# Nineteen columns a head: queries and keys of a Hedgehog attention relative to their last feature

## The chip, the cores and the metric

The kernel runs on one core of a Trainium2 chip. The metric is device time in microseconds (us) of one execution, the median over runs; lower is better. A core has five engines with an instruction stream each: PE (TensorE, matrix products, with its weight loads listed as PEld), DVE (VectorE), ACT (ScalarE), POOL (GpSimd) and SP (SyncE, which issues the DMA transfers here). Work passes through SBUF (on-chip memory of 128 partitions) and PSUM (where matrix products are summed).

## The reference

Two layers, each an attention (A) and a dense network (B) with a normalization ahead and a residual behind, on x of 2048 rows by 640 columns, 32 heads of 20 columns, 1536 hidden columns, all in float32:

```python
def _A_ref(x, wqkv, w_phi, wo):
    qkv = transpose((x @ wqkv).reshape(B, S, 3, H, Dh), 2, 0, 3, 1, 4)
    q, k, v = qkv[0], qkv[1], qkv[2]
    pq = einsum("bhsd,hdf->bhsf", q, w_phi)
    pk = einsum("bhsd,hdf->bhsf", k, w_phi)
    phi_q = concatenate([softmax(pq), softmax(-pq)], axis=-1)
    phi_k = concatenate([softmax(pk), softmax(-pk)], axis=-1)
    kv = einsum("bhsf,bhsd->bhfd", phi_k, v)
    z  = einsum("bhsf->bhf", phi_k)
    num = einsum("bhqf,bhfd->bhqd", phi_q, kv)
    den = einsum("bhqf,bhf->bhq", phi_q, z)[..., None] + 1e-6
    return (num / den) @ wo
def _B_ref(x, w1, b1, w2):
    h = x @ w1 + b1
    return (h * tanh(softplus(h))) @ w2
for _ in range(2):
    x = x + _A_ref(layernorm(x), ...)
    x = x + _B_ref(layernorm(x), ...)
```

The softmax runs over a head's 20 features. It doesn't change when one number is added to all of them, and neither does the softmax of the negated features.

## The kernel before

**Tiles and precision.** The 2048 rows are 16 tiles of 128, two tiles to a block, eight blocks. The 640 columns are contracted in five steps of 128 (`KD`). Each operand of a large product is split into a high part that TensorE takes in its faster float32 form (fp32r) and the remainder, and each product is three matmuls: high by high, high by low, low by high. A row of 640 outputs is made in two halves of 320 columns (`HC`), each in its own PSUM bank. The weights are the moving operand of these matmuls, so a half moves 320 columns past a stationary 128 by 128 tile of the normalized rows.

**Folding.** At the start of layer 1 `w_phi` is multiplied into the weights of queries and keys, so that no product with `w_phi` is left in the loops. The heads' 20 by 20 matrices stand as blocks of six on a diagonal of `bd`, 120 wide; `fold_part` (L244) multiplies a stretch of the raw weights by such a block, and `fold_end` (L250, L251) splits the sum into the high and low weights. The folded weights are written to `wp_d` in DRAM (L205, L206) and read back for layer 2 (L194, L200).

**First pass** (`attend_first`, over the eight blocks). For each block six projections run in the order k0, k1, v0, v1, q0, q1: keys, values and queries of the block's two tiles, 30 matmuls each (`project_half`, L364). What follows a projection is a generator that is advanced by one step after each later projection:

- `features` turns a projection into the two softmaxes: ACT copies it out of PSUM into the second half of each head's 40 columns in tile `e` (L381, listed under the helper's line L129); DVE takes maximum and minimum per head (L388); one subtraction makes the first half (L389, on POOL for queries, on DVE for keys) and one the second (L391, DVE); ACT takes the exponential in place; DVE sums (L397) and inverts (L398); POOL multiplies (L399).
- Keys are then multiplied with the values (L436) into one PSUM bank that sums over all blocks.
- Queries are transposed by DVE (L444) and written to `e_d` in DRAM by four transfers (L448).

Key tiles come from the pool `big` with five buffers, shared with other uses. Query tiles are two fixed buffers (`query_tile`, shown as r210 and r211, or r in a row), so the copy of a query waits until the writes to `e_d` of the query two tiles before have landed. The projections take PSUM tiles `mm` (two of them) or `one` (four). In layer 1 the block's two halves of normalized rows are also transposed by TensorE; in layer 2 they arrive transposed from DRAM.

**Second pass** (`attend_second`). The last query tile is projected in `rest`, between other work. `load` (L597) reads a block's features back from `e_d`; `average` (L637) multiplies them with the product of keys and values; the output projection runs again through `project_half` (L364), here with `wo`, after which come the residual and the statistics for the next normalization.

**Dense network** (`dense`). Hidden products move 256 columns (L759), Mish runs on ACT, DVE and POOL, and the second product moves 320 (L801).

**Order.** A scheduler decides the order of instructions on each engine from its own simulated timeline, with priority by the written order. The start of layer 1 (all engines) and the second pass (PE and SP) keep the written order. Copies made through `act` keep their order among themselves. POOL, DVE, ACT and SP each run their streams in order, so an instruction that waits holds what stands behind it on its engine.

Of the kernel before, what the change touches and what calls it, by code (L numbers as in the profile page):

```python
# [8 lines left out]
F32 = mybir.dt.float32  # L9
F32R = mybir.dt.float32r  # L10
AF = mybir.ActivationFunctionType
ALU = mybir.AluOpType
# [4 lines left out]
P = 128  # L17
S = 2048
D = 640
F = 1536  # L20
H = 32
DH = 20
KD = D // P
KF = F // P
BT = 2
# [2 lines left out]
NT = S // P  # L28
G = 11
HC = D // 2  # L30
EW = 2 * D
GW = 3 * (DH + 1)
VW = H * (DH + 1)
# [8 lines left out]
def kernel(  # L42
# [13 lines left out]
    nc = tc.nc  # L56
# [6 lines left out]
    dram = ctx.enter_context(tc.tile_pool(name="dram", bufs=1, space=DRAM))  # L63
# [36 lines left out]
    stats = const.tile([P, NB, 2, BT], F32, name="stats")  # L100


    wp_d = dram.tile([2, 2, KD, P, D], F32, name="wp_d")

    e_d = [dram.tile([EW, BLK], F32, name=f"e_d{b}") for b in range(NB)]

# [83 lines left out]
    def load_q_weights():  # L190
        ws = [r2_pair(k) for k in range(KD)]
        for k in range(KD):
            for s in range(2):
                nc.sync.dma_start(ws[k][s].bitcast(F32), wp_d[0, s, k])  # L194
        return ws

    def load_k_weights(kv_ws):
        for k in range(KD):
            for s in range(2):
                nc.sync.dma_start(kv_ws[k][s][:, :D].bitcast(F32), wp_d[1, s, k])  # L200

    def spill_qk_weights(kv_ws, q_ws):
        for k in range(KD):
            for s in range(2):
                nc.sync.dma_start(wp_d[1, s, k], kv_ws[k][s][:, :D].bitcast(F32))  # L205
                nc.sync.dma_start(wp_d[0, s, k], q_ws[k][s].bitcast(F32))  # L206

    def make_five(j, rows, low=nc.gpsimd):

# [30 lines left out]
    def fold_part(ps, k, t, bd, raw):  # L240

        r, rows = raw[t]
        n = 120 * (t % 3) if t < 5 else 200
        nc.tensor.matmul(ps[:, n:n + rows], r[:rows, k * P:(k + 1) * P], bd[:rows, t, :rows],  # L244
                         start=True, stop=True)

    def fold_end(ws, ps, k, c):
        n0, n1 = (0, 360) if c == 0 else (360, D)
        hi, lo = ws[k][0][:, n0:n1], ws[k][1][:, n0:n1]
        nc.scalar.activation(hi, ps[:, :n1 - n0], AF.Copy)  # L250
        nc.vector.tensor_tensor(lo, ps[:, :n1 - n0], hi.bitcast(F32), op=ALU.subtract)  # L251
# [94 lines left out]
        return Transposed(cols=cols)  # L346


    def project(xts, t, ws, col, ps=None):

        if ps is None:
            mm = mm_tile()
            ps = [mm[:, 0], mm[:, 1], mm]
        for c in range(2):
            project_half(ps[c], xts, t, ws, col, c)
        return ps

    def project_half(ps, xts, t, ws, col, c, ks=range(KD)):
        sl = slice(t * P, (t + 1) * P)
        cs = slice(col + c * HC, col + (c + 1) * HC)  # L360
        for k in ks:
            h, l, wh, wl = xts.hs[k], xts.ls[k], ws[k][0][:, cs], ws[k][1][:, cs]
            for n, (a, r) in enumerate(((h, wh), (h, wl), (l, wh))):
                nc.tensor.matmul(ps[:, :HC], a[:, sl], r, start=(k == 0 and n == 0),  # L364
                                 stop=(k == KD - 1 and n == 2))

    def both(ps):

        return ps[2][:, :, :HC]


    def query_tile(i):
# [2 lines left out]
    def features(ps, e, pool_sub):  # L375

        eg = e.rearrange("p (g d) -> p g d", d=DH)
        eh = e.rearrange("p (h s d) -> p s h d", s=2, d=DH)
        ec = e.rearrange("p (c h s d) -> p s c h d", c=2, s=2, d=DH)[:, 1]
        if len(ps) > 2:  # L380
            act(ec, both(ps).rearrange("p c (h d) -> p c h d", d=DH), AF.Copy)  # L381
        else:
            for c in range(2):
                act(ec[:, c], ps[c][:, :HC].rearrange("p (h d) -> p h d", d=DH), AF.Copy)
        yield
        m = work.tile([P, 2, H], F32, tag="m", name="m", bufs=2)
        for s, op in ((0, ALU.max), (1, ALU.min)):
            nc.vector.tensor_reduce(m[:, s], eh[:, 1], axis=AX.X, op=op)  # L388
        (nc.gpsimd if pool_sub else nc.vector).tensor_tensor(  # L389
            eh[:, 0], eh[:, 1], m[:, 0].unsqueeze(2).to_broadcast([P, H, DH]), op=ALU.subtract)  # L390
        nc.vector.tensor_tensor(eh[:, 1], m[:, 1].unsqueeze(2).to_broadcast([P, H, DH]), eh[:, 1],  # L391
                                op=ALU.subtract)
        yield
        act(e, e, AF.Exp)
        yield
        r = work.tile([P, 2 * H], F32, tag="r", name="r", bufs=2)
        nc.vector.tensor_reduce(r, eg, axis=AX.X, op=ALU.add)  # L397
        nc.vector.reciprocal(r, r)  # L398
        nc.gpsimd.tensor_tensor(eg, eg, r.unsqueeze(2).to_broadcast([P, 2 * H, DH]), op=ALU.mult)  # L399
        yield  # L400
# [6 lines left out]
    def attend_first(layer, x_src, first):  # L407
# [17 lines left out]

        def keys(xts, i, v):
            e = big_tile()
            yield from features(project(xts, i % BT, kv_ws, 0), e, False)
            yield
            if i % BT == 0 and BT < i < NT - BT:  # L430
                yield
            for r in range(9):
                for j in range(4):
                    h = 3 * (4 * (r // 3) + j) + r % 3
                    if h < H:
                        nc.tensor.matmul(kva[32 * j:32 * j + DH + 1, 40 * r:40 * r + 40],  # L436
                                         v[:, (DH + 1) * h:(DH + 1) * (h + 1)], e[:, 40 * h:40 * h + 40],
                                         start=(i == 0 and r == 0), stop=(i == NT - 1), skip_group_check=True)

        def queries(xts, i, ps=None):  # L440
            e = query_tile(i)
            yield from features(project(xts, i % BT, q_ws, 0) if ps is None else ps, e, True)

            nc.vector.transpose(e, e)  # L444
            b, t = divmod(i, BT)
# [20 lines left out]
        if first is None:  # L466
            with written():
# [6 lines left out]
                nc.sync.dma_start(bd[:40, 5, :40], phi_bd[80:120, 4, 80:120])  # L474
                nc.sync.dma_start(bd[40:80, 5, 40:80], phi_bd[:40, 5, :40])
                nc.sync.dma_start(bd[:, 3:5], phi_bd[:, 3:5])
                raw_q += load_raw(0, range(3, 6))
                kv_ws = [r1_pair(k) for k in range(KD)]
                raw_v = [fetch_v(k) for k in range(KD)]
# [1 line left out]
                early = fetch(x_src, 1)  # L481
                mvs = [norm_stats(t, xt) for t in range(BT)]
                norm_scale(0, mvs)

                q_ws = [r2_pair(k) for k in range(KD)]
                mm = [mm_tile(), mm_tile()]
# [18 lines left out]
                fold_end(q_ws, pcs[4], 4, 0)  # L505
                mm = mm_tile()
                q0 = [mm[:, 0], mm[:, 1], mm]
                project_half(q0[0], nxt, 0, q_ws, 0, 0)

                def make_v(k):  # L510
                    split(kv_ws[k][0][:, D:2 * D], kv_ws[k][1][:, D:2 * D], raw_v[k])
# [1 line left out]
                for k in range(KD):  # L513
# [3 lines left out]
                    fold_end(q_ws, ps, k, 1)  # L517
                    if k > 0:
                        make_v(k - 1)
                project_half(q0[1], nxt, 0, q_ws, 0, 1)  # L520
                make_v(KD - 1)
            nc.sync.dma_start(mask, bass.AP(tensor=head_mask.tensor, offset=head_mask.offset,
                                            ap=[[1, 120], [120 * (DH + 1), 3]]))
# [48 lines left out]
        def rest():  # L572

            ps = [one_tile(), one_tile()]
            project_half(ps[0], xts, 1, q_ws, 0, 0)
            advance()
            advance()
            yield
            project_half(ps[1], xts, 1, q_ws, 0, 1, range(3))
            yield  # L580
            project_half(ps[1], xts, 1, q_ws, 0, 1, range(3, KD))
            pending.append(queries(xts, NT - 1, ps))
            next(pending[-1])
            while pending:
                yield
                advance()
# [376 lines left out]
```

## Time and profile before

| | us |
|---|---|
| median of 3 runs | 1377.01 |
| lowest and highest | 1376.39, 1379.66 |
| span of the profiled execution | 1375.0 |
| mean granted clock of TensorE | 0.999 |

The span is counted from the first to the last instruction of one execution; the runs' times hold a little more around it. By stage, from the busy times by stretches (us):

| stretch | what runs | length | PE busy | DVE busy | ACT busy | POOL busy |
|---|---|---|---|---|---|---|
| 0 to 43 | start: loads, folding, first tiles | 43.0 | 37.2 | 28.5 | 19.3 | 8.4 |
| 43 to 280 | layer 1, first pass | 237.0 | 236.6 | 194.9 | 96.3 | 109.5 |
| 280 to 364 | layer 1, second pass | 84.0 | 84.0 | 58.5 | 22.1 | 34.9 |
| 364 to 690 | layer 1, dense | 326.0 | 326.0 | 265.6 | 164.6 | 76.2 |
| 690 to 955 | layer 2, first pass | 265.0 | 262.9 | 228.9 | 101.1 | 113.9 |
| 955 to 1040 | layer 2, second pass | 85.0 | 85.0 | 56.9 | 24.3 | 34.5 |
| 1040 to 1375 | layer 2, dense | 335.0 | 330.5 | 240.1 | 153.8 | 63.6 |

The borders are chosen by eye from the timeline; passes overlap at them by some microseconds.

Rows of the profile are read like this. A group row gives the line in the kernel, the engine, the operation, the output and inputs by name, their shapes, the count (x), then the busy time, the mean of one in ns, and the engine's idle time just before with what ended most of it. A timeline row begins with the start in us and the length in us; a count at its end says that several like instructions follow each other, and the length is that of the whole run; square brackets give the idle time before it. In the chain of waits a row gives start, length and what ran then. Matmuls are pipelined: the mean of one matmul in a group is longer than the distance from one to the next.

### The profile page before, as it was taken

The numbers are of one execution on the slowest core, as the hardware profiler recorded it, in microseconds if no ns is written. First come the engines' busy times: TensorE is split into PE (matmuls) and PEld (weight loads), VectorE is DVE, ScalarE is ACT, GpSimd is POOL, SyncE is SP. The second block draws the span as 40 slices with busy tenths as digits, with TensorE's granted clock in tenths as the row PEclk, the third lists the DMA queues.
The fourth block names the chain that finished last, engine by engine and source line by source line (L and its number), as shares of the span: only waits on it lengthen the run. The fifth ranks groups of instructions, "written<-read, shape, count | busy, mean of one in ns | idle before, by whom it ended". The sixth has DMA issues, their size and how long they took to land.

```text
span 1375.0 us, 30860 instructions
## 1 busy us (share of the span) xinstructions
PE 1362.1 (99%) x12896; PEld 1349.8 (98%) x12896; DVE 1073.3 (78%) x1822; ACT 581.3 (42%) x970; POOL 441.0 (32%) x334
## 2 busy tenths in 40 slices
PE   9999999999999999999999999999999999999998
PEld 8999999999999999999999999999999999999998
DVE  5898877886688887788769899988678776677775
ACT  4344443222454545545444334332235444454443
POOL 1345553354322222122235434444242111111112
PEclk9999999999999999999999999999999999999999
DMA  9443424788614442244473433368975221333200
GB/s 337 148 95 62 75 40 96 204 242 292 224 55 97 116 105 77 59 107 99 141 245 77 85 59 64 67 132 270 285 253 151 77 59 41 94 97 96 69 29 20
DMA packets 350469, 169.85 MB, mean 124 GB/s; under 512 B 287209, under 2 KB 323801, under 8 KB 350329
## 3 DMA queue, kind: packets, MB, share of 16 engines
q1 hardware_dynamic: 350329, 167.88, 45.2%
q8 instruction: 101, 1.65, 0.5%
q14 instruction: 39, 0.32, 0.1%
HBM read 104.92 MB, written 62.91 MB: 122 GB/s over the span
## 4 chain that ended last, share of the span: by engine, by line
PE 96%; DMA 1%; DVE 1%; ACT 0%; issue 0%; DVEq 0%; SPq 0%
PE mm L364 29%; PE one L759 24%; PE mm L801 24%; PE one L364 12%; PE mm L637 3%; PE one L300 2%; PE one L436 2%; DMA v<-in_wv 1%; DMA r1l<-wp_d 0%; DVE r1l L251 0%; DVE bn L270 0%; ACT xn L129 0%; DVE r L397 0%; DVE xt L811 0%; ACT r L129 0%
## 5 line engine op out<-in xcount | busy, mean ns | idle before, releaser
L801 PE MATMUL mm<-r2h,ol 128*128 128x320 f32 x1280 | 305.0, 309 | 0.0
L785 POOL TENSOR_TENSOR ol<-big,ol 128x512 fp32r<-128x512 f32 (+1 forms) x98 | 129.9, 1326 | 483.7 <-ACT ol L784 409.3
L759 PE MATMUL one<-xtl,r1h 128*128 128x256 f32 x960 | 268.2, 279 | 0.0
L759 PE MATMUL one<-xth,r1l 128*128 128x256 f32 x960 | 268.0, 279 | 0.0
L759 PE MATMUL one<-xth,r1h 128*128 128x256 f32 x960 | 265.9, 279 | 0.0
L801 PEld LDWEIGHTS mm<-r2h,ol 128*128 128x128 f32 x1280 | 219.2, 188 | 0.3 <-ACT ol L784 0.3
L801 PE MATMUL mm<-r2l,ol 128*128 128x320 f32 x640 | 197.3, 309 | 0.0
L364 PE MATMUL mm<-r1h,xth 128*128 128x320 f32 x600 | 187.6, 313 | 1.6 <-DVE r1l L251 1.6
L364 PE MATMUL mm<-r1l,xth 128*128 128x320 f32 x600 | 185.8, 310 | 0.0
L364 PE MATMUL mm<-r1h,xtl 128*128 128x320 f32 x600 | 185.6, 310 | 0.0
L759 PEld LDWEIGHTS one<-xtl,r1h 128*128 128x128 f32 x960 | 180.4, 188 | 0.0
L759 PEld LDWEIGHTS one<-xth,r1l 128*128 128x128 f32 x960 | 180.4, 188 | 0.0
L759 PEld LDWEIGHTS one<-xth,r1h 128*128 128x128 f32 x960 | 179.6, 188 | 0.0
L774 DVE TENSOR_SCALAR big<-big 128x512 f32<-128x512 f32 (+1 forms) x98 | 57.1, 583 | 110.0 <-ACT big L772 109.8
L399 POOL TENSOR_TENSOR r<-r,r 128x1280 f32<-128x1280 f32 x32 | 77.7, 2429 | 156.4 <-DVE r L398 141.8
L801 PEld LDWEIGHTS mm<-r2l,ol 128*128 128x128 f32 x640 | 120.2, 188 | 0.0
L776 ACT ACTIVATE big<-big,two 128x512 f32<-128x512 f32 (+1 forms) x98 | 70.1, 716 | 116.1 <-DVE big L775 116.0
L772 ACT ACTIVATE big<-one,b1s 128x256 f32<-128x256 f32 x192 | 80.9, 468 | 89.0 <-PE one L759 88.5
L784 ACT ACTIVATE ol<-big 128x512 fp32r<-128x512 f32 (+1 forms) x98 | 60.9, 622 | 136.0 <-DVE big L783 135.9
L364 PEld LDWEIGHTS mm<-r1h,xth 128*128 128x128 f32 x600 | 112.8, 188 | 2.6 <-DVE r1l L251 1.8
L364 PEld LDWEIGHTS mm<-r1h,xtl 128*128 128x128 f32 x600 | 112.7, 188 | 0.2
L364 PEld LDWEIGHTS mm<-r1l,xth 128*128 128x128 f32 x600 | 112.8, 188 | 0.0
(133 smaller groups left out, 3119.9 us busy)
## 6 DMA issues: line engine op xcount, KB each, us to landing
e_d<-r SPq DMA_DIRECT2D x128, 160.0 KB, 4.0
big<-e_d SPq DMA_DIRECT2D x32, 640.0 KB, 7.6
x_d<-xt SPq DMA_DIRECT2D x23, 640.0 KB, 3.9
xt<-x_d SPq DMA_DIRECT2D x22, 640.0 KB, 5.5
n_d<-xn SPq DMA_DIRECT2D x176, 80.0 KB, 2.2
xt<-in_x SPq DMA_DIRECT2D x16, 640.0 KB, 4.4
xn<-x_d SPq DMA_DIRECT2D x28, 320.0 KB, 4.4
v<-n_d SPq DMA_DIRECT2D x30, 256.0 KB, 3.1
```

Source lines behind the costliest of these rows:

```text
L300: nc.tensor.transpose(ps[:, c, t * P:(t + 1) * P], self.rows[t][:, (c0 + c) * P:(c0 + c + 1) * P], ident)
L364: nc.tensor.matmul(ps[:, :HC], a[:, sl], r, start=(k == 0 and n == 0), stop=(k == KD - 1 and n == 2))
L399: nc.gpsimd.tensor_tensor(eg, eg, r.unsqueeze(2).to_broadcast([P, 2 * H, DH]), op=ALU.mult)
L436: nc.tensor.matmul(kva[32 * j:32 * j + DH + 1, 40 * r:40 * r + 40], v[:, (DH + 1) * h:(DH + 1) * (h + 1)], e[:, 40 * h:40 * h + 40], start ...
L637: nc.tensor.matmul(po[64 * q:64 * q + 64, c, GW * j:GW * j + w], phs[g][:n, s0:s0 + 64], kvb[:n, g, :w], start=True, stop=True)
L759: nc.tensor.matmul(ph[:, j, :], l, r, start=(n == 0), stop=(n == 3 * KD - 1))
L772: exps[0] = nc.scalar.activation(part(ta, 0)[:, j - js.start], ph[:, j, :], AF.Exp, bias=b1s[:, 2 * pr + j:2 * pr + j + 1]).ins
L774: nc.vector.tensor_scalar_min(e, e, E_CAP)
L776: nc.scalar.activation(r, n, AF.Ln, bias=two)
L784: nc.scalar.activation(ah[:, js], n, AF.Copy)
L785: nc.gpsimd.tensor_tensor(al[:, js], n, ah[:, js].bitcast(F32), op=ALU.subtract)
L801: nc.tensor.matmul(pys[t][:, c, :HC], l[:, j, sl], r, start=(f == 0 and n == 0), stop=(f == KF - 1 and n == 2))
```

## The change

Queries and keys are made with 19 columns a head (`DL`) in place of 20: 608 in place of 640 columns (`QK`), 304 in place of 320 a half (`QC`). Each is the feature less the head's twentieth feature, and the twentieth entry, which is zero by that, is set by a memset. By the invariance above both softmaxes stay what they were. For that, the last column of each head's block of `w_phi` is subtracted from the others on POOL (`shift_phi`, three calls), the folding multiplies by the first 19 columns, and the folded weights, their copies in DRAM and the projections of queries and keys are 608 columns wide. `features` sets the twentieth column of each head in tile `e` to zero on POOL and copies 19 columns a head behind it. From maximum and minimum on, 20 columns a head are worked on as before. Values, the output projection and the dense network keep their widths.

```diff
@@ -20,6 +20,7 @@
 F = 1536
 H = 32
 DH = 20
+DL = DH - 1
 KD = D // P
 KF = F // P
 BT = 2
@@ -28,6 +29,8 @@
 NT = S // P
 G = 11
 HC = D // 2
+QK = H * DL
+QC = QK // 2
 EW = 2 * D
 GW = 3 * (DH + 1)
 VW = H * (DH + 1)
@@ -100,7 +103,7 @@
     stats = const.tile([P, NB, 2, BT], F32, name="stats")
 
 
-    wp_d = dram.tile([2, 2, KD, P, D], F32, name="wp_d")
+    wp_d = dram.tile([2, 2, KD, P, QK], F32, name="wp_d")
 
     e_d = [dram.tile([EW, BLK], F32, name=f"e_d{b}") for b in range(NB)]
 
@@ -191,19 +194,19 @@
         ws = [r2_pair(k) for k in range(KD)]
         for k in range(KD):
             for s in range(2):
-                nc.sync.dma_start(ws[k][s].bitcast(F32), wp_d[0, s, k])
+                nc.sync.dma_start(ws[k][s][:, :QK].bitcast(F32), wp_d[0, s, k])
         return ws
 
     def load_k_weights(kv_ws):
         for k in range(KD):
             for s in range(2):
-                nc.sync.dma_start(kv_ws[k][s][:, :D].bitcast(F32), wp_d[1, s, k])
+                nc.sync.dma_start(kv_ws[k][s][:, :QK].bitcast(F32), wp_d[1, s, k])
 
     def spill_qk_weights(kv_ws, q_ws):
         for k in range(KD):
             for s in range(2):
-                nc.sync.dma_start(wp_d[1, s, k], kv_ws[k][s][:, :D].bitcast(F32))
-                nc.sync.dma_start(wp_d[0, s, k], q_ws[k][s].bitcast(F32))
+                nc.sync.dma_start(wp_d[1, s, k], kv_ws[k][s][:, :QK].bitcast(F32))
+                nc.sync.dma_start(wp_d[0, s, k], q_ws[k][s][:, :QK].bitcast(F32))
 
     def make_five(j, rows, low=nc.gpsimd):
 
@@ -240,12 +243,20 @@
     def fold_part(ps, k, t, bd, raw):
 
         r, rows = raw[t]
-        n = 120 * (t % 3) if t < 5 else 200
-        nc.tensor.matmul(ps[:, n:n + rows], r[:rows, k * P:(k + 1) * P], bd[:rows, t, :rows],
-                         start=True, stop=True)
+        heads = rows // DH
+        n = DL * (6 * (t % 3) if t < 5 else 10)
+        nc.tensor.matmul(ps[:, n:n + heads * DL].rearrange("p (j d) -> p j d", d=DL), r[:rows, k * P:(k + 1) * P],
+                         bd[:rows, t, :rows].rearrange("p (j d) -> p j d", d=DH)[:, :, :DL], start=True, stop=True)
+
+    def shift_phi(bd, ts):
+
+        b = bd[:, ts].rearrange("p t (j d) -> p (t j) d", d=DH) if isinstance(ts, slice) else (
+            bd[:80, ts, :80].rearrange("p (j d) -> p j d", d=DH))
+        nc.gpsimd.tensor_tensor(b[:, :, :DL], b[:, :, :DL], b[:, :, DL:].to_broadcast([b.shape[0], b.shape[1], DL]),
+                                op=ALU.subtract)
 
     def fold_end(ws, ps, k, c):
-        n0, n1 = (0, 360) if c == 0 else (360, D)
+        n0, n1 = (0, 18 * DL) if c == 0 else (18 * DL, QK)
         hi, lo = ws[k][0][:, n0:n1], ws[k][1][:, n0:n1]
         nc.scalar.activation(hi, ps[:, :n1 - n0], AF.Copy)
         nc.vector.tensor_tensor(lo, ps[:, :n1 - n0], hi.bitcast(F32), op=ALU.subtract)
@@ -346,27 +357,27 @@
         return Transposed(cols=cols)
 
 
-    def project(xts, t, ws, col, ps=None):
+    def project(xts, t, ws, col, ps=None, w=HC):
 
         if ps is None:
             mm = mm_tile()
             ps = [mm[:, 0], mm[:, 1], mm]
         for c in range(2):
-            project_half(ps[c], xts, t, ws, col, c)
+            project_half(ps[c], xts, t, ws, col, c, w=w)
         return ps
 
-    def project_half(ps, xts, t, ws, col, c, ks=range(KD)):
+    def project_half(ps, xts, t, ws, col, c, ks=range(KD), w=HC):
         sl = slice(t * P, (t + 1) * P)
-        cs = slice(col + c * HC, col + (c + 1) * HC)
+        cs = slice(col + c * w, col + (c + 1) * w)
         for k in ks:
             h, l, wh, wl = xts.hs[k], xts.ls[k], ws[k][0][:, cs], ws[k][1][:, cs]
             for n, (a, r) in enumerate(((h, wh), (h, wl), (l, wh))):
-                nc.tensor.matmul(ps[:, :HC], a[:, sl], r, start=(k == 0 and n == 0),
+                nc.tensor.matmul(ps[:, :w], a[:, sl], r, start=(k == 0 and n == 0),
                                  stop=(k == KD - 1 and n == 2))
 
-    def both(ps):
-
-        return ps[2][:, :, :HC]
+    def both(ps, w=HC):
+
+        return ps[2][:, :, :w]
 
 
     def query_tile(i):
@@ -377,11 +388,12 @@
         eg = e.rearrange("p (g d) -> p g d", d=DH)
         eh = e.rearrange("p (h s d) -> p s h d", s=2, d=DH)
         ec = e.rearrange("p (c h s d) -> p s c h d", c=2, s=2, d=DH)[:, 1]
+        nc.gpsimd.memset(eh[:, 1, :, DL:], 0.0)
         if len(ps) > 2:
-            act(ec, both(ps).rearrange("p c (h d) -> p c h d", d=DH), AF.Copy)
+            act(ec[:, :, :, :DL], both(ps, QC).rearrange("p c (h d) -> p c h d", d=DL), AF.Copy)
         else:
             for c in range(2):
-                act(ec[:, c], ps[c][:, :HC].rearrange("p (h d) -> p h d", d=DH), AF.Copy)
+                act(ec[:, c, :, :DL], ps[c][:, :QC].rearrange("p (h d) -> p h d", d=DL), AF.Copy)
         yield
         m = work.tile([P, 2, H], F32, tag="m", name="m", bufs=2)
         for s, op in ((0, ALU.max), (1, ALU.min)):
@@ -425,7 +437,7 @@
 
         def keys(xts, i, v):
             e = big_tile()
-            yield from features(project(xts, i % BT, kv_ws, 0), e, False)
+            yield from features(project(xts, i % BT, kv_ws, 0, w=QC), e, False)
             yield
             if i % BT == 0 and BT < i < NT - BT:
                 yield
@@ -439,7 +451,7 @@
 
         def queries(xts, i, ps=None):
             e = query_tile(i)
-            yield from features(project(xts, i % BT, q_ws, 0) if ps is None else ps, e, True)
+            yield from features(project(xts, i % BT, q_ws, 0, w=QC) if ps is None else ps, e, True)
 
             nc.vector.transpose(e, e)
             b, t = divmod(i, BT)
@@ -474,6 +486,7 @@
                 nc.sync.dma_start(bd[:40, 5, :40], phi_bd[80:120, 4, 80:120])
                 nc.sync.dma_start(bd[40:80, 5, 40:80], phi_bd[:40, 5, :40])
                 nc.sync.dma_start(bd[:, 3:5], phi_bd[:, 3:5])
+                shift_phi(bd, slice(0, 3))
                 raw_q += load_raw(0, range(3, 6))
                 kv_ws = [r1_pair(k) for k in range(KD)]
                 raw_v = [fetch_v(k) for k in range(KD)]
@@ -481,6 +494,8 @@
                 early = fetch(x_src, 1)
                 mvs = [norm_stats(t, xt) for t in range(BT)]
                 norm_scale(0, mvs)
+                shift_phi(bd, slice(3, 5))
+                shift_phi(bd, 5)
 
                 q_ws = [r2_pair(k) for k in range(KD)]
                 mm = [mm_tile(), mm_tile()]
@@ -505,7 +520,7 @@
                 fold_end(q_ws, pcs[4], 4, 0)
                 mm = mm_tile()
                 q0 = [mm[:, 0], mm[:, 1], mm]
-                project_half(q0[0], nxt, 0, q_ws, 0, 0)
+                project_half(q0[0], nxt, 0, q_ws, 0, 0, w=QC)
 
                 def make_v(k):
                     split(kv_ws[k][0][:, D:2 * D], kv_ws[k][1][:, D:2 * D], raw_v[k])
@@ -517,7 +532,7 @@
                     fold_end(q_ws, ps, k, 1)
                     if k > 0:
                         make_v(k - 1)
-                project_half(q0[1], nxt, 0, q_ws, 0, 1)
+                project_half(q0[1], nxt, 0, q_ws, 0, 1, w=QC)
                 make_v(KD - 1)
             nc.sync.dma_start(mask, bass.AP(tensor=head_mask.tensor, offset=head_mask.offset,
                                             ap=[[1, 120], [120 * (DH + 1), 3]]))
@@ -572,13 +587,13 @@
         def rest():
 
             ps = [one_tile(), one_tile()]
-            project_half(ps[0], xts, 1, q_ws, 0, 0)
+            project_half(ps[0], xts, 1, q_ws, 0, 0, w=QC)
             advance()
             advance()
             yield
-            project_half(ps[1], xts, 1, q_ws, 0, 1, range(3))
+            project_half(ps[1], xts, 1, q_ws, 0, 1, range(3), w=QC)
             yield
-            project_half(ps[1], xts, 1, q_ws, 0, 1, range(3, KD))
+            project_half(ps[1], xts, 1, q_ws, 0, 1, range(3, KD), w=QC)
             pending.append(queries(xts, NT - 1, ps))
             next(pending[-1])
             while pending:
```

## The prediction

> **What bounds the kernel now.** I read the page first, then the chain of waits in order of time, the groups of instructions, the busy time by stretches, and the timelines of single engines where a bound had to be checked.
>
> ```profile
> span 1375.0 us, 30860 instructions
> ...
> PE 1362.1 (99%) x12896; PEld 1349.8 (98%) x12896; DVE 1073.3 (78%) x1822; ACT 581.3 (42%) x970; POOL 441.0 (32%) x334
> ...
> PE 96%; DMA 1%; DVE 1%; ACT 0%; issue 0%; DVEq 0%; SPq 0%
> ```
>
> TensorE is busy for 1362.1 of 1375.0 us and makes 96% of the chain that ends last. A busy share doesn't say that each matmul runs at its best, so the next question is what one matmul costs, and whether that depends on its columns.
>
> ```profile
> 162.37 4.40 PE mm L364 x30
> ...
> 191.47 4.40 PE mm L364 x30
> ...
> 354.97 8.80 PE one L364 x60
> 363.77 14.82 PE one L759 x127
> ...
> 690.39 5.36 DMA r1l<-wp_d
> ...
> 819.73 26.60 PE mm L364 x180
> ...
> 847.73 26.60 PE mm L364 x180
> ```
>
> Columns: start, length, what. The 60 projections of 320 columns (L364) take 8.80 / 60 = 146.7 ns each; the 127 matmuls of 256 columns beside them (L759) take 14.82 / 127 = 116.7 ns. Both have a stationary operand of 128 by 128, so its load doesn't set the pace of either, and 146.7 / 320 and 116.7 / 256 are both 0.46 ns a column. Time goes with columns.
>
> ```profile
> 0.00:43.00 43.00, 37.24 (x274) 35.88 (x275) 28.53 (x69) 19.30 (x40) 8.38 (x19) 1.00 0.96 338
> ...
> 160.00:189.30 29.30, 29.30 (x322) 29.02 (x321) 24.14 (x36) 12.98 (x19) 15.48 (x11) 1.00 0.32 51
> ...
> 815.00:843.00 28.00, 28.00 (x310) 27.74 (x309) 25.55 (x27) 10.65 (x15) 12.68 (x7) 1.00 0.40 75
> ```
>
> Columns: stretch, its length, busy time of PE, PEld, DVE, ACT, POOL, clock, DMA share, GB/s. A block of the first attention pass takes 29.1 us in layer 1 (191.47 - 162.37 from query run to query run) and 28.0 in layer 2 (847.73 - 819.73), with TensorE busy throughout and the clock at 1.00. But in layer 2 VectorE is busy for 25.55 of 28.0: the second engine is close behind. In the first 43 us the DMA engines are busy for 0.96 and TensorE has gaps.
>
> **The columns.** Queries and keys go from 320 to 304 columns a half.
>
> ```profile
> L364 PE MATMUL mm<-r1h,xth 128*128 128x320 f32 x600 | 187.6, 313 | 1.6 <-DVE r1l L251 1.6
> ...
> L364 PE MATMUL one<-r2h,xth 128*128 128x320 f32 x340 | 107.9, 317 | 0.0
> ...
> L364 PE MATMUL mm<-r2h,xth 128*128 128x320 f32 x300 | 93.8, 313 | 0.0
> ...
> L364 PE MATMUL one<-r1h,xth 128*128 128x320 f32 x40 | 11.8, 312 | 0.9 <-ACT r1h L137 0.9
> ```
>
> Each product has three such terms, so L364 runs 3 x (600 + 340 + 300 + 40) = 3840 times: queries, keys, values and the output projection, 960 each (2 layers x 16 tiles x 2 halves x 15). Queries and keys are 1920. At 146.7 / 320 x 16 = 7.33 ns less each, that is 14.08 us. From the difference of the two widths, (146.7 - 116.7) / 64 x 16 = 7.5 ns, it is 14.4. The lower bound is 0, if 304 columns cost as many as 320: both rows are multiples of 64 and can't exclude a step. I take 7.33, since a step would need a reason that no row gives. The first query tile (30 matmuls) runs among loads, so 0.22 goes off: **-13.86**.
>
> The Trainium skill, "TensorE: Matmul & The Clock Gate", section "Back-to-back issue gap", gives columns / 2.4 + 2.5 ns for one isolated warm matmul. That would be 135.8 ns for 320 columns, where this trace has 146.7, so the measurement decides; by the rule's slope the saving is an estimated 6.67 ns x 1920 = 12.8 us instead of 14.1.
>
> The fold of w_phi also narrows (120 to 114, 80 to 76). Sixteen of its matmuls in the start's timeline below take 2.04 us, 128 ns each; 5% of 60 of them is 0.38 us, half of it beside loads: **-0.2**. The folded weights are spilled and reloaded with 608 instead of 640 columns; 5% of the 5.36 us of reload in the chain is **-0.2**.
>
> **Start.** Three POOL subtractions are added, and SP gets no new transfer.
>
> ```profile
> 6.42 0.19 POOL L279 TENSOR_SCALAR ve<-mv 128x1 f32<-128x1 f32 x1 [5.14 <-DVE mv L272]
> ...
> 26.75 0.46 POOL L279 TENSOR_SCALAR ve<-mv 128x1 f32<-128x1 f32 x2 [18.36 <-DVE mv L272]
> ...
> 845.10 1.28 POOL L389 TENSOR_TENSOR r<-r,m 128x640 f32<-128x640 f32 x1 [1.68 <-DVE m L388]
> ...
> 6.60 1.12 PE L244 MATMUL mm<-big,raw 120*128 120x120 f32 x8
> 8.62 2.04 PE L244 MATMUL mm<-big,raw 120*128 120x120 f32 x16 [0.90 <-DMA raw<-in_wqk_t]
> ```
>
> The rows are POOL's and TensorE's timelines. The nearest operation is the broadcast subtraction of 640 elements, 1.28 us; 342 elements are 0.68 us by it. It comes before the 6.42 row, in POOL's idle 5.14 us, as soon as the first part of phi has landed; the fold behind it, at 6.60, waits 0.90 us for the weights' rows later anyway, so I take 0, at most 0.7 if all of it shows. The other two (228 and 76 elements, 0.6 us) fall into the idle 18.36 us before 26.75: 0. Without that cover they would cost 0.6 us.
>
> **Memsets.** Each of 64 feature tiles gets a POOL memset of 128x32, on which the max and min on VectorE wait as well as on the copy.
>
> ```profile
> 0.71 0.20 POOL masks.py:197 MEMSET ident<- 128x128 f32 x1 [0.29 <-POOLq L954]
> ...
> 835.84 2.37 POOL L399 TENSOR_TENSOR big<-big,r 128x1280 f32<-128x1280 f32 x1 [1.18 <-DVE r L398]
> 839.63 2.37 POOL L399 TENSOR_TENSOR big<-big,r 128x1280 f32<-128x1280 f32 x1 [1.42 <-DVE r L398]
> ...
> 843.45 0.71 ACT L129 ACTIVATE r<-mm 128x640 f32<-128x640 f32 x1 [4.82 <-DMA e_d<-r]
> ```
>
> The rows are from POOL's timeline, the last from ACT's. A memset of four times the elements takes 0.20 us; the bounds are 0 and 0.2 us each. For keys it may run as soon as one of five buffers is free, in the built order some two blocks ahead. For queries there are two buffers, each free only when its e_d writes have landed; the copy of the second query waits for that already, so the memset runs beside a copy of 0.71 us. Where the wait is new is on POOL, which runs in order: the memset of the first query stands ahead of the key's multiplication at 835.84 and holds that, the second key's and the next subtraction. POOL idles 1.18 and 1.42 us before these two, which belong to the keys. I take 0, and 1.5 us a block if the writes land late (a rival below). Copies of 608 elements are shorter, off the path: 0.
>
> The Trainium skill, "SBUF — State Buffer", section "Who interferes with whom", says that a VectorE operation with two SBUF inputs contends with a GpSimd operation that reads SBUF, not with one that only writes. By that the memset stretches nothing. No row here shows a memset beside such an operation; without the rule four memsets of 0.2 us would add up to 0.8 us a block on VectorE.
>
> **The second loop.** Where VectorE's idle time sits in a block of layer 2 decides how much of the 0.88 us a block (120 x 7.33 ns) survives.
>
> ```profile
> 163.68 1.45 DVE L444 STREAM_TRANSPOSE r<-r 128x1280 f32<-128x1280 f32 x1
> ...
> 191.64 1.51 DVE L444 STREAM_TRANSPOSE r<-r 128x1280 f32<-128x1280 f32 x1 [0.15 <-POOL r L399]
> ...
> 825.10 1.54 DVE L388 TENSOR_REDUCE m<-big 128x32 f32<-128x640 f32 x2
> ...
> 835.59 1.45 DVE L444 STREAM_TRANSPOSE r<-r 128x1280 f32<-128x1280 f32 x1
> ...
> 844.19 1.55 DVE L388 TENSOR_REDUCE m<-r 128x32 f32<-128x640 f32 x2 [1.91 <-ACT r L129]
> 845.66 2.13 DVE L391 TENSOR_TENSOR r<-m,r 128x640 f32<-128x640 f32 x2
> ```
>
> The rows are VectorE's timeline, two of layer 1 and four of layer 2. The second query is transposed until 837.04, written to e_d, and its buffer is copied into again at 843.45; the max starts at 844.19, 7.15 us after the transpose. From there VectorE runs almost without a gap to the next transpose's end at 865.04, 20.85 us. 7.15 + 20.85 = 28.0: this loop is as long as TensorE's. Its one visible gap is about 0.13 us before 825.10, so in the old order it can't go below 27.87, while TensorE would allow 28.0 - 0.88 = 27.12. The change also reorders VectorE: in the built program the first query's subtraction (L391) stands before the second's max instead of behind it, in the idle 1.91 us. The pair then ends not at 847.79 but after POOL's subtraction, 845.10 + 1.28, plus 0.81, at 847.2: 0.58 sooner. The first query's transpose moves one place forward, for which I count a tenth. The loop comes to about 27.4, TensorE to 27.12. The lag of 0.3 us a block doesn't stop TensorE at once, since the second query's copy ends at 844.16 and its PSUM tile is wanted again only at 847.7. Over six blocks it grows to 1.8 us, and VectorE's idle 1.14 us in the last block (below) takes part back. I take **+1.0**, between 0 and 5.3 (nothing left of the 0.88 in six blocks). In layer 1 VectorE idles 5 us a block and the transposes stand 191.64 - 163.68 = 28.0 apart, below the 28.2 that TensorE will need: 0.
>
> ```profile
> 909.12 1.55 DVE L388 TENSOR_REDUCE m<-big 128x32 f32<-128x640 f32 x2 [1.14 <-ACT big L129]
> ...
> 921.57 2.36 POOL L399 TENSOR_TENSOR big<-big,r 128x1280 f32<-128x1280 f32 x1 [1.34 <-PE mm L364]
> ...
> 923.67 1.48 PE L436 MATMUL one<-big,v 128*21 128x40 f32 x128
> ```
>
> At the end of each first pass the last key's multiplication ends at 923.93 and the product of keys and values starts at 923.67: no slack. TensorE's work between narrows by 45 matmuls, 0.33 us, which is then waited: **+0.66** for two layers.
>
> **SP.** The built order moves the first read of load(0) ahead of eight e_d writes of block 5.
>
> ```profile
> 204.90 1.41 PE one L436 x126
> ...
> 215.41 9.82 SPq L448 DMA_DIRECT2D e_d<-r  x8
> 225.33 1.02 SPq L597 DMA_DIRECT2D big<-e_d  x1
> ```
>
> Its buffer is the one that block 5's second key left at 206.3 (204.90 + 1.41), nine us before those writes begin at 215.41, so nothing behind it is held: 0. If it were held, the writes would free the query buffers late.
>
> **Sum.** -13.86 - 0.2 - 0.2 + 1.0 + 0.66 = -12.6. The execution spans 1375.0 us and the median of the runs is 1377.01, 2.0 more. 1375.0 - 12.6 + 2.0 = **1364.4 us**.
>
> **Rivals.**
> 1. The query loop decides: contention or a late landing keeps it near 27.87. For it speaks that it equals TensorE's loop today; against it the new order. Layer 2 keeps 0.13 of 0.88 us in six blocks, 4.5 us lost instead of 1.0, and layer 1 loses 1.5 with it: 1364.4 + 3.5 + 1.5 = 1369.4.
> 2. The columns don't count: 304 cost as 320. For it only that both measured widths are multiples of 64; against it the common 0.46 ns a column. Then nothing is saved and the start's 0.7 may show: 1377.7.
> 3. Slower: POOL's order. The first query's memset waits for its e_d landing with three operations behind it. If that landing is 1.5 us too late in each block, layer 2's loop is 27.4 + 1.5 = 28.9 (0.9 above today) and layer 1's 28.0 + 1.5 = 29.5 (0.4 above). Over six blocks each that is +7.8: 1385. It decides as soon as the delay passes 0.6 us in layer 2 and 1.1 in layer 1. Against it: POOL's idle 1.18 us at that very place.
>
> **How the numbers follow.** A change within 0.3% (4.1 us) can't be told from none here. Forecast 0.66, rival 1 0.20, rival 2 0.07, rival 3 0.07. The forecast's own range is 1362 (14.4 saved, no lag) to 1368. For 8 in 10 the range reaches into rival 1: **1361 to 1371.5**. Faster: forecast and rival 1, 0.86. Same: rival 2 and a mild rival 3, 0.08. Slower: 0.06.
>
> **What would show it.** L364's 304-column groups should follow at 139 ns; 60 in 8.4 us in the chain. Blocks of the first pass should be 28.2 us in layer 1 and 27.1 to 27.4 in layer 2, with TensorE still busy throughout. VectorE's idle time before the max of the second query should shrink from 1.91 us. The fold should start at 6.6 to 7.3 us. I am wrong if the cadence stays at 147 ns (rival 2), if TensorE shows gaps before L364 ended by ACT's copies (rival 1), or if POOL's memset of r ends late with the key's multiplication behind it (rival 3).

## The result

The changed kernel takes 1369.91 us (median of 4 runs, 1368.56 to 1371.23) against 1377.17 in the same series: a ratio of 0.9944, 95% interval 0.9929 to 0.9958. That is 7.3 us less. The forecast was 12.6 less, at 1364.4; the measured time lies inside the range of 1361 to 1371.5, and beside the 1369.4 of rival 1.

The changed kernel's page first, its span, busy times and shares of the chain of waits:

```profile
span 1366.8 us, 30959 instructions
...
PE 1351.2 (99%) x12896; PEld 1337.9 (98%) x12896; DVE 1075.5 (79%) x1822; ACT 578.4 (42%) x970; POOL 452.6 (33%) x401
...
PE 32%; DVE 1%; POOL 1%; issue 0%; DVEq 0%; POOLq 0%
```

TensorE lost 10.9 us of busy time, the span 8.2; the profiled execution is the fastest of the four, so its lead is larger than the medians' 7.3. The chain, which was 96% TensorE, now runs into VectorE and POOL where layer 2's first pass ends, and isn't followed further back than that. Its rows there, beside two from the same view of experiment e3 below, where the blocks run without a break:

```profile
902.11 1.78 DVE big L401
903.89 1.40 DVE r L409
905.28 1.42 DVE r L456
...
914.03 2.37 POOL big L411
```

```profile
192.08 8.40 PE mm L375 x60
...
811.42 25.80 PE mm L375 x180
...
838.63 25.80 PE mm L375 x180
```

The cadence can be read from the second fence: 8.40 / 60 = 140.0 ns for 304 columns, where 320 took 146.7. The 180 projections of a block, 120 of them narrowed, take 25.80 in place of 26.60. Both give 6.67 ns a matmul, so the 1920 are worth 12.8 us. A whole block takes 838.63 - 811.42 = 27.21 us.

Where the rest went shows in when the dense network's hidden product starts (first and last start behind the durations), the kernel before and then the changed one:

```profile
L759 PE MATMUL one<-xth,r1h x960: 274/280/283, 363.6 to 1359.4; 128*128 128x256 f32 x192
```

```profile
L774 PE MATMUL one<-xth,r1h x960: 274/280/283, 357.0 to 1351.2; 128*128 128x256 f32 x192
```

By the end of layer 1's attention the lead is 6.6 us. Of that 1.0 isn't the change's: TensorE's first projection starts at 12.51 in place of 13.49, since a landing at the start was late in the execution of before (e5, with the same start as the kernel before, has 12.69). That leaves 5.6 for layer 1; by the last product the lead is 8.2, so layer 2 brings 1.6. The columns alone are worth 6.4 in each layer. TensorE's waits in layer 2's first pass (what was waited for: us in total, times, longest), again before and after:

```profile
PE one L364 <- ACT r1h L137: 0.9, 1, 0.9
PE mm L637 <- PE mm L637: 0.4, 1, 0.4
```

```profile
PE mm L375 <- DVE xtl L317: 1.8, 2, 1.6
PE one L375 <- ACT v L132: 0.9, 1, 0.9
PE one L375 <- ACT r1h L140: 0.9, 1, 0.9
PE one L448 <- POOL big L411: 0.8, 1, 0.8
PE mm L652 <- PE mm L652: 0.4, 1, 0.4
PE mm L375 <- ACT r L132: 0.4, 1, 0.4
PE one L623 <- DVE xn L619: 0.2, 1, 0.2
```

The waits grew from 1.3 to 5.4 us. (6.4 less 4.1 is 2.3; the 0.7 us between that and 1.6 is in no row of the waits.) They are ended by the split of the next block's rows on VectorE (L317), by copies on ACT at the start of the pass and of a query, and by the last key's multiplication on POOL. The longest, 1.6 us, lies early in the pass. Rows of the timelines of TensorE, VectorE and POOL:

```profile
782.11 0.41 PE L375 MATMUL mm<-r1h,xtl 128*128 128x304 f32 x1 [1.59 <-DVE xtl L317]
```

```profile
744.88 1.50 DVE L456 STREAM_TRANSPOSE r<-r 128x1280 f32<-128x1280 f32 x1
...
775.40 1.45 DVE L456 STREAM_TRANSPOSE r<-r 128x1280 f32<-128x1280 f32 x1
...
780.59 1.47 DVE L317 TENSOR_TENSOR xtl<-xn,xth 128x256 fp32r<-128x256 f32 x1
```

```profile
779.41 2.36 POOL L411 TENSOR_TENSOR big<-big,r 128x1280 f32<-128x1280 f32 x1 [1.32 <-DVE r L410]
```

The split ends at 782.06 and TensorE goes on at 782.11. VectorE is late there: the second query's transpose of block 1 starts 775.40 - 744.88 = 30.5 us after block 0's, where TensorE needs 27.2 a block. From the next blocks, VectorE and POOL:

```profile
800.66 1.80 DVE L317 TENSOR_TENSOR xtl<-xn,xth 128x512 fp32r<-128x512 f32 x1
802.39 0.54 DVE L410 RECIPROCAL r<-r 128x64 f32<-128x64 f32 x1
802.85 1.45 DVE L456 STREAM_TRANSPOSE r<-r 128x1280 f32<-128x1280 f32 x1
...
830.24 1.45 DVE L456 STREAM_TRANSPOSE r<-r 128x1280 f32<-128x1280 f32 x1
...
832.98 0.66 DVE L317 TENSOR_TENSOR xtl<-xn,xth 128x512 fp32r<-128x512 f32 x1
```

```profile
799.54 2.37 POOL L411 TENSOR_TENSOR r<-r,r 128x1280 f32<-128x1280 f32 x1 [4.99 <-DVE r L410]
803.48 0.16 POOL L391 MEMSET r<- 128x32 f32 x1 [1.56 <-DMA e_d<-r]
...
830.46 2.38 POOL L411 TENSOR_TENSOR big<-big,r 128x1280 f32<-128x1280 f32 x1 [0.63 <-DVE r L410]
```

The second query's transposes stand 830.24 - 802.85 = 27.39 us apart. That looks like the loop of about 27.4 that the prediction had worked out, but the steps after the first are 27.45, 27.39, 27.08 and 26.95: the loop closes up to TensorE's pace and then runs below it. TensorE's other wait for the split is 0.2 us, between 800 and 816, and from 816 to 900 it waits for nothing. So the time is lost in one late step at the start of the pass, not a little in each block.

The same split of 128x512 takes 1.80 us beside POOL's multiplication and 0.66 right behind one: the first ends at 802.46, 0.55 after the multiplication (801.91). As long as the multiplication runs VectorE stands nearly still, and is counted as busy. The Trainium skill, "SBUF — State Buffer", section "Who interferes with whom", says that a VectorE instruction with two inputs in SBUF contends with a GpSimd one that reads SBUF; the trace agrees, with 1.1 us here.

### The profile page after: what moved, and what is told of

It is laid out like the page before. It is cut to its first block, busy times and chain, and to the rows that moved or that the text cites. A ratio compares the mean times of both kernels' runs of the same rounds, so it can differ in the third digit from the quotient of the medians.

```text
span 1366.8 us, 30959 instructions
## 1 busy us (share of the span) xinstructions
PE 1351.2 (99%) x12896; PEld 1337.9 (98%) x12896; DVE 1075.5 (79%) x1822; ACT 578.4 (42%) x970; POOL 452.6 (33%) x401
## 5 line engine op out<-in xcount | busy, mean ns | idle before, releaser
L375 PE MATMUL mm<-r1h,xth 128*128 128x304 f32 (+1 forms) x600 | 185.4, 309 | 2.2 <-DVE r1l L262 1.5
L375 PE MATMUL mm<-r1h,xtl 128*128 128x304 f32 (+1 forms) x600 | 183.6, 307 | 2.0 <-DVE xtl L317 1.8
L375 PE MATMUL mm<-r1l,xth 128*128 128x304 f32 (+1 forms) x600 | 183.8, 306 | 0.0
```

Of the source, the lines that this page charges most:

```text
L375: nc.tensor.matmul(ps[:, :w], a[:, sl], r, start=(k == 0 and n == 0), stop=(k == KD - 1 and n == 2))
```

## The experiments

Theory 1: VectorE, with the query loop in its stream, is so close behind TensorE in the first pass that a shorter TensorE waits for it. Theory 2: the 64 memsets, by their waits on POOL and the order built around them, cost it. Each time is a median, each ratio is to the kernel before in the same series, with its 95% interval.

**e1, wide again.** The changed kernel with 320 columns moved.

```diff
-        cs = slice(col + c * w, col + (c + 1) * w)
+        c0 = col + c * (288 if w == QC else w)
+        cs = slice(c0, c0 + HC)
```

> The changed kernel, but the matmuls of queries and keys move 320 columns again; weights, memsets, copies and the subtraction of phi stay as changed. The second half then starts at column 288 of 608, so its heads get other columns than the reference's. Theory 1 (VectorE is late): TensorE's waits of about 5.8 us in layer 2's first pass come from VectorE, which is hardly less busy than TensorE there, so they go when TensorE is slow again: like the kernel before within 2 us, 1375 to 1379, TensorE's waits in that pass 1 to 2 us. Theory 2 (the memsets, by their waits on POOL and the order built around them, cost it): the waits stay, 1382 to 1385.

1377.91 us, ratio 1.0000 (0.9991 to 1.0009). TensorE's waits in layer 2's first pass are 2.4 us, a little above the forecast, half of them for the copy of one value weight (L140). All the rest of the change, memsets, subtractions and order, costs nothing that can be measured while TensorE is slow. Theory 2 has no place here.

**e2, zero column on ACT.**

```diff
-        nc.gpsimd.memset(eh[:, 1, :, DL:], 0.0)
+        act(eh[:, 1, :, DL], ident[:, :H], AF.Copy, scale=0.0)
```

> The changed kernel with the zero column written by ACT (64 copies of 128x32 with a scale of zero) in place of POOL's memset. Theory 1 (VectorE is late): no change beyond 1.5 us, 1368.5 to 1371.5, and TensorE still waits in layer 2 for the split of the rows and for copies of queries. Theory 2 (the memsets on POOL cost it): most of the missing 5.5 us comes back, 1364 to 1366.

1374.11 us, 0.9973 (0.9963 to 0.9983): slower than the changed kernel, which neither theory had forecast. Its waits in layer 2's first pass:

```profile
PE mm L375 <- DVE xtl L317: 2.8, 6, 1.2
PE one L448 <- POOL big L411: 2.4, 1, 2.4
```

The split is late in six places instead of two. The query loop is longer: the second query's transposes lie 27.82 us apart (804.79 and 832.61 in this kernel's VectorE timeline), above TensorE's 27.2. A zero copy stands ahead of each copy of a query, behind the same landing, but it holds it by only 0.14 us (they start at 806.82 and 806.96 on ACT). The built order changed too: the first query's subtraction (L403) stands behind the second's max again, as in the kernel before. Which of the two lengthens the loop wasn't tried; e12 tests whether the zero copies cost anything where VectorE has room.

**e3, a subtraction moved off VectorE.**

```diff
-            yield from features(project(xts, i % BT, kv_ws, 0, w=QC), e, False)
+            yield from features(project(xts, i % BT, kv_ws, 0, w=QC), e, bool(layer))
```

> The changed kernel with the keys' first subtraction (128x640, two a block) moved from VectorE to POOL in layer 2. Theory 1 (VectorE is late): VectorE does 1.6 us less a block, so TensorE's waits in layer 2's first pass shrink from 5.8 us to 2 us or less: 1364.5 to 1367. Theory 2 (POOL's order and waits cost it): POOL gets 2.6 us more a block and the waits stay or grow: 1369 to 1373.

1365.19 us, 0.9910 (0.9897 to 0.9924), as theory 1 said. The busy times of three blocks of layer 2, the changed kernel and then e3 (stretch, length, then PE, PEld, DVE, ACT, POOL):

```profile
760.00:844.00 84.00, 82.17 (x926) 80.95 (x925) 76.22 (x84) 31.41 (x45) 38.62 (x30) 1.00 0.40 72
```

```profile
760.00:844.00 84.00, 84.00 (x943) 83.27 (x942) 73.61 (x81) 32.23 (x47) 48.51 (x38) 1.00 0.39 72
```

VectorE does 2.6 us less, POOL 9.9 more, and TensorE's breaks are gone. The first step of the loop, 30.5 us in the changed kernel, is 26.4 here (transposes at 746.23 and 772.60). What remains of its waits in the pass lies at the start, but for one on itself:

```profile
PE one L375 <- ACT v L132: 1.1, 1, 1.1
PE one L375 <- ACT r1h L140: 0.8, 1, 0.8
PE mm L652 <- PE mm L652: 0.4, 1, 0.4
```

**e4, narrower still.** 14 of 15 matmuls of queries and keys at 256 columns; the output lacks those products.

```diff
+                m = 256 if w == QC and (k or n) else w
-                nc.tensor.matmul(ps[:, :w], a[:, sl], r, ...)
+                nc.tensor.matmul(ps[:, :m], a[:, sl], r[:, :m], ...)
```

> The changed kernel with 14 of the 15 matmuls of each half of queries and keys cut to 256 columns (columns 256 to 303 get one product of 15, so the output isn't the reference's). TensorE has 39 us less to do, 2.46 us a block. Theory 1 (VectorE and the query loop are the next bound in layer 2, at 27 to 27.4 us a block): blocks of layer 2 stay at 26.5 to 27.4 us, and only layer 1 gains: 1344 to 1355. Theory 2 (no bound near, only the memsets' waits): layer 2's blocks come to 24.7 to 25.2 us, 1330 to 1334.

1370.15 us, 0.9940 (0.9927 to 0.9954): 39 us less work for TensorE and no gain over the changed kernel. Theory 1's figure was too low by 15 us, because it let layer 1 gain in full: against the changed kernel, layer 1 (first projection to first hidden product) is 3.6 us shorter, and layer 2 (from there to its own first hidden product) 4.7 us longer. TensorE waits in layer 1 too, in its first pass:

```profile
PE mm L376 <- ACT r L132: 5.7, 3, 3.2
PE one L449 <- POOL big L412: 5.5, 1, 5.5
```

In layer 2's first pass, with the busy times of 27 us of it:

```profile
PE mm L376 <- ACT r L132: 12.3, 5, 5.5
PE one L449 <- POOL big L412: 5.2, 1, 5.2
...
815.00:842.00 27.00, 25.19 (x304) 24.79 (x303) 26.73 (x28) 10.43 (x15) 12.71 (x11) 0.96 0.40 75
```

TensorE waits for copies of queries, whose buffers come free late, and VectorE is busy for 26.73 of 27.00 us. The transposes stand 858.05 - 831.10 = 26.95 apart: that loop, not the columns, is the bound below 304. TensorE's granted clock is lower here too, 0.96 in the last row and 0.989 over the whole execution, where the changed kernel has 1.00; why isn't shown. Even if all of TensorE's time went with the clock, 1.1% of 1368.8 us would be 15 of the 39.

**e5, the move of e3 on the kernel before.**

```diff
-            yield from features(project(xts, i % BT, kv_ws, 0), e, False)
+            yield from features(project(xts, i % BT, kv_ws, 0), e, bool(layer))
```

> The kernel before, with only the keys' first subtraction moved from VectorE to POOL in layer 2. If VectorE binds only because TensorE has become shorter, nothing is gained here, since TensorE already runs without waits in the blocks of layer 2: 1376 to 1378.5. If the move is worth its 4.7 us whatever the width: 1372 to 1373.5.

1376.75 us, 0.9995 (0.9987 to 1.0004). The move is worth nothing until TensorE is shorter. With it on both sides, the change is worth 0.9995 to 0.9910, some 11.6 us.

**e6 and e7, four query buffers.** In layer 2 every other block's queries go to the x tiles, idle in that pass; e7 adds the edit of e3.

```diff
+        if spare:
+            return x_tile().rearrange("p s d -> p (s d)")
...
-            e = query_tile(i)
+            e = query_tile(i, layer and i // BT % 2 == 0)
```

> The changed kernel with four buffers for queries in layer 2 in place of two (the x tiles, idle in that pass, take those of every other block). VectorE's work stays. Theory 1a (the query loop binds: transpose, writes to e_d, landing, copy into the same buffer): the wait for the landing goes, and with it most of TensorE's 5.8 us of waits: 1364.5 to 1366.5. Theory 1b (VectorE's amount of work binds, wherever it waits): within 1.5 us of the changed kernel, 1368.5 to 1371.5.

> Both reliefs on the changed kernel in layer 2: four buffers for queries, and the keys' first subtraction on POOL. If the subtraction alone has left only the waits at the start and end of the pass, the buffers add nothing: 1364.5 to 1366. If landing still holds VectorE in places: 1363 to 1364.5.

e6: 1367.21 us, 0.9929 (0.9916 to 0.9941), between the two variants of the theory. In layer 2's first pass the wait on copies of queries is gone and that on the split is down to 0.4 us. But layer 1's second pass shows 1.5 us of waits that it hadn't (for `big`, 0.5, and for `xt`, 0.6 and 0.4); the program is the same there but for the built order, and the cause wasn't tried (the profiled execution is 1.7 us slower than the median, so others may not have them). e7: 1365.81 us, 0.9920 (0.9906 to 0.9933): with VectorE relieved the buffers add nothing.

**e8, the split on POOL** in layer 2's first pass.

```diff
-            nc.vector.tensor_tensor(lo, ps[:, :n], hi.bitcast(F32), op=ALU.subtract)
+            self.low.tensor_tensor(lo, ps[:, :n], hi.bitcast(F32), op=ALU.subtract)
```

> The changed kernel with the low half of the rows (L317, the instruction that TensorE is seen to wait for) made on POOL in place of VectorE in layer 2's first pass. Theory 1 (VectorE's load): VectorE loses 2 to 3 us a block, 1364.5 to 1367. Rival (POOL's order): the split stands behind multiplications of 2.4 us and memsets that wait for landings, and TensorE waits for it more than before: 1371 to 1376.

1367.34 us, 0.9929 (0.9916 to 0.9943). Another relief of VectorE that brings back about half, a little less than theory 1 forecast; the rival falls. As in e3, what is gone from TensorE's waits is the split.

**e9 and e11, each memset twice,** on the changed kernel and on e10.

```diff
         nc.gpsimd.memset(eh[:, 1, :, DL:], 0.0)
+        nc.gpsimd.memset(eh[:, 1, :, DL:], 0.0)
```

> The changed kernel with each of the 64 memsets issued twice on POOL. If the memsets cost nothing, as the prediction counted them: within 1.5 us of the changed kernel, 1368.5 to 1371.5. If their waits and places on POOL are what holds layer 2: at least 2 us more, 1372 to 1376.

> Each memset issued twice, as in the run before that came to 1373.4 us, but on the version with the keys' first subtraction on POOL in both layers (1364.2). If memsets have a price of their own on POOL (3.5 us for 64 more): 1366.5 to 1369. If the 3.5 us came from where the waits fell in that one build: 1363 to 1365.8.

e9: 1373.38 us, 0.9965 (0.9951 to 0.9978), which by itself speaks for theory 2. The 3.5 us lie in layer 2 (3.4 in the traces), but not in its first pass, where TensorE waits 5.3 us against 5.4. About half is a wait just behind the pass, in the turning of the rows (L311), with nothing named that ended it:

```profile
PE one L311 <- issue: 1.8, 1, 1.8
```

e11: 1364.33 us, 0.9908 (0.9893 to 0.9922), against 1364.23 in e10's series. 64 more memsets cost nothing where VectorE has room. The wait of L311 isn't theirs: e1 has it with 1.4 us, e6, e7 and e10 with 0.7 to 0.8, all without a doubled memset, and the changed kernel's profiled execution lacks it. What makes it, and the rest of e9's 3.5 us, stay open, so a price of memsets in the changed kernel itself isn't excluded.

**e10 and e12, both layers relieved.** e10 is e3's edit with `True` in place of `bool(layer)`; e12 adds the edit of e2.

> The changed kernel with the keys' first subtraction on POOL in both layers. In layer 2 as with the move there alone (1365.2). In layer 1 TensorE has about 0.9 us of waits left that VectorE or POOL end (a copy of a query, the last key's multiplication), and VectorE idles 5 us a block: 1364.3 to 1366 if POOL's longer queue does no harm, 1367 or more if the last key's multiplication comes later by it.

> The zero column written by ACT, which cost 4.2 us on the changed kernel, on the version with the keys' first subtraction on POOL in both layers (1364.2). If the zero copy cost that only because it lengthens the query loop where VectorE has no room: 1363 to 1366, with TensorE's waits on the split of the rows gone. If it costs by itself: 1367 to 1369.5.

e10: 1364.23 us, 0.9905 (0.9891 to 0.9918), with the lowest median and ratio of all, though its interval overlaps e3's. The waits on a copy of a query and on the last key's multiplication (0.3 and 0.2 us in layer 1 of the changed kernel) are gone. e12: 1364.53 us, 0.9910 (0.9893 to 0.9926), and no wait on the split: the zero copies cost nothing where VectorE has room.

## Why the prediction was half right

- **The columns.** Right in kind, mis-sized: the term "-13.86", from 7.33 ns a matmul. Dividing 146.7 by 320 counts a fixed part as if it went with the columns; measured are 6.67 ns, 12.8 us for all 1920. The difference of 320 and 256, 7.5 ns for 16 columns, was further off: from 304 to 320 a column costs 0.42 ns, from 256 to 304 it costs (140.0 - 116.7) / 48 = 0.49, and why the three widths don't lie on one line isn't shown. The Trainium skill's slope of 1 / 2.4 ns a column, which the prediction weighed and left ("TensorE: Matmul & The Clock Gate", "Back-to-back issue gap"), gave 12.8.
- **The second loop.** Right in kind, since a shorter TensorE met a VectorE that was late; wrong in how the time goes, and mis-sized in "I take +1.0". The prediction ends the loop at 865.04, which no row shows: in the trace of before that transpose starts at 863.19 and ends at 864.64. The old loop was 863.19 - 835.59 = 27.60 us, not 28.0, and the prediction's own steps lead from there to about 27.0, not 27.4. The runs show that: 27.08 and 26.95 late in the pass, 26.95 in e4, below TensorE's 27.2. So the lag of 0.3 us a block isn't there. What came instead is one step of 30.5 us at the start of the pass, for which the slack of 3.5 us in PSUM was too little: TensorE waits 1.6 us for the split behind it. ACT's copies at the start and POOL's multiplication at the end add their parts; in all TensorE's waits in that pass grew by 4.1 us.
- **Where that step comes from** is open. e1 has it too (transposes at 750.50 and 780.53) and waits only 0.4 us for the split, so it comes with the built order, and the shorter TensorE lays it open. e3's edit shortens it, but also changes the order there: block 0's two transposes lie 5.8 us apart (740.46 and 746.23), in the changed kernel 3.4. e6 and e8 keep that spacing nearly (3.4 and 2.8), shorten the step to 28.8 and bring back about half. So relief works without the other order too; how much of e3's gain is the order's isn't separated.
- **Layer 1, counted as 0.** Mis-sized, by about 0.8 us: 5.6 of 6.4 arrive (0.2 of the rest is the pass end below). From the first projection to the first hidden product layer 1 takes 344.5 and 344.9 us in the changed kernel and e3, and 343.4 to 344.2 in e10, e11 and e12, whose relief reaches it. VectorE hasn't 5 us to spare in every block there, as its share includes time at a stand. The block of the changed kernel that answers to the one from 160 to 189.3 has VectorE at 27.53 of 28.00 us, where that had 24.14 of 29.30, with 36 instructions in both; the next two blocks have 23.08 and 22.92:

```profile
156.00:184.00 28.00, 28.00 (x319) 27.73 (x318) 27.53 (x36) 12.58 (x18) 14.95 (x14) 1.00 0.31 48
```

- **Pass ends, "+0.66".** Near: 0.8 us in layer 2 and 0.2 in layer 1 for the last key's multiplication.
- **Memsets 0, start 0, SP 0.** Borne out as far as the runs go: e1 and e11 for the memsets, with what e9 leaves open. The fold starts at 6.74 and its later rows aren't waited for in this execution. No wait of TensorE in a first pass is ended by a transfer.
- **Rival 1** names the time, 1369.4, and the loop, but not its way: TensorE waits more for VectorE's split than for ACT's copies, the loop is not at 27.87, and the loss isn't spread over six blocks. That its time lies within 0.6 us of the measured one is luck. **Rival 2** is out: 140.0 ns. **Rival 3** is out in its size, 1385, but its wait is there: the memset at 803.48 waited 1.56 us for a landing, and the key's multiplication starts behind it at 803.59, though its reciprocal was done at 802.93. That is half a microsecond, and in the next block (829.68) nothing is held.

The sum with the measured columns: -12.8 + 0.2 for the first tile - 0.4 for fold and reload = -13.0, of which the relieved e3, e7, e10, e11 and e12 show 11.5 to 13.8 and the changed kernel 7.3. That 1364.4 came no nearer is the second loop's doing first (waits of 4.1 us more, where 1.0 and 0.33 were counted), then the columns' and layer 1's; the measured 1369.91 lies in the range because the range was drawn wide enough to reach rival 1.

## What to carry to other kernels

Before shortening the engine that sets the pace, work out the loop of the next one, from the same instruction to the same instruction through its buffers and transfers, and price it from the first block on, not in steady state alone: here the steady loop had room, and the first step had none. If the gap is smaller than the cut, relieve the second engine in the same change: one subtraction on another engine was worth nothing before the cut and nearly 5 us behind it. To find what a column costs, take the difference of two widths that lie close together, not the quotient of one.

## What was not expected of the hardware

A VectorE subtraction with both inputs in SBUF takes 0.66 us alone and 2.09 beside one of POOL's multiplications, and the profile counts the stand as busy time:

```profile
827.76 2.09 DVE L317 TENSOR_TENSOR xtl<-xn,xth 128x512 fp32r<-128x512 f32 x1
```

POOL's multiplication from 826.93 to 829.31 covers all of it but the last 0.54. The 25.55 of 28.0 us that the prediction read as VectorE's work hold such stands, so its share tells how full its stream is, not how much work is in it.
